# Reordering pair products and operand sums in blocks 1 to 3 and 6 of an attention and GeGLU kernel

## The chip, the core and the metric

The kernel runs on one core of one Trainium2 chip. The metric is the device time of one execution in microseconds; lower is better. Before the change it is 294.11 us, the median of three runs (294.11 to 294.32). The profile of one such run spans 292.1 us from its first to its last instruction.

## What is computed

Linear attention over 8 batches, 8 heads, 576 positions and a head width of 64, followed by a gated feed-forward layer on 4608 rows:

```python
q_s = softmax(q, over the head width)
k_s = softmax(k, over the positions)
kv  = einsum('bhsd,bhse->bhde', k_s, v)
x   = einsum('bhsd,bhde->bhse', q_s, kv)      # reshaped to 4608 x 512
g   = x @ w_gate                              # 512 x 1536
val = x @ w_val                               # 512 x 1536
out = (gelu(g) * val) @ w_out                 # 1536 x 512
```

## The kernel before

A batch is a **block** of 512 rows; the remaining 64 rows of all eight batches are gathered into block 8 (`B`). The blocks run in the order 0 to 6, 8, 7. While the feed-forward of block b runs on TensorE (PE), the attention of block b + 1 is prepared on the other engines: DVE (VectorE), ACT (ScalarE) and POOL (GpSimd).

From block 2 on, most of `x @ w_gate` and `x @ w_val` is done as a Strassen-Winograd scheme: the rows of x are cut into two halves of 256, and two columns of 128 hidden units, k and k + 3, form a **pair**. Seven products of four 128x256 matmuls take the place of eight. A column that is not in a pair is done plainly, as two **halves** (`g` and `v`) of four 128x512 matmuls. The scheme needs four sums of x (`xs`), four of the weights, and, for the output product, sums of the hidden values (`sh`, `s4` and in place in `ht`).

The order of one block is a string. `k.i` is step i of pair k, `8g` and `8v` are the two halves of column 8, letters are places where other work rides along:

```python
FOUR = ("a 7g l 7v n 0.1 6.1 0.2 6.2 0.3 6.3 m p 10g 0.4 6.4 1.1 t 10v 1.2 s0 8g u0 1.3 8v 1.4 2.1"
        " 11g 2.2 11v 2.3 s1")                                 # blocks 2, 3: four pairs
FIVE = ("a 8g l 8v n m 0.1 6.1 0.2 6.2 0.3 6.3 0.4 1.1 p 6.4 7.1 t 1.2 7.2 1.3 s0 7.3 2.1 1.4 u0 11g 2.2"
        " y 7.4 11v 2.3 s1")                                   # blocks 4 to 6: five pairs
SIX = ("0.1 6.1 0.2 6.2 0.3 6.3 0.4 1.1 6.4 7.1 s0 1.2 7.2 1.3 u0 7.3 1.4 2.1 7.4 8.1 2.2"
       " 8.2 2.3 s1 8.3 2.4")                                  # blocks 8, 7: six pairs
```

The four steps of a pair use three PSUM tiles, `pga`, `pgb` and `pgc`. What reads a tile has to be done before the next product is added to it:

```python
if i == 1:
    product_gv(1, pa, ...)          # PE
    nc.scalar.copy(out=pb, in_=pa)  # ACT: seed of pb
    product_gv(5, pc, ...)
    s5 = snap(pc, b >= B - 1 or b > 3 and k % NO == 1)   # on DVE if true, else ACT
elif i == 2:
    product_gv(6, pa, ...)          # adds to pa: waits for the seed copy
    s2 = snap(pa)                   # ACT
    product_gv(3, pc, ...)          # adds to pc: waits for s5
    add(cc[:, 0], pc, s2)           # DVE
elif i == 3:
    product_gv(7, pa, ...)          # waits for s2
    add(cc[:, 1], pa, s5)           # DVE
    product_gv(2, pb, ...)
    final(pb, k)                    # ACT gelu, then DVE product into ht
    ... upper(cc)                   # ACT gelu, then POOL (for pair 8 DVE) product into ht
else:
    product_gv(4, pa, ...)          # waits for add(cc[:, 1], pa, s5)
    final(pa, k + 3)
```

The sums of x are four chained subtractions on POOL: `t0 = b12 - b11`, `t1 = b22 - t0`, `t2 = b22 - b12`, `t3 = b21 - t1`. Product 5 reads `t0`, product 6 `t1`, product 7 `t2` and product 4 `t3`; products 1, 2 and 3 read x itself.

The places `a` and `n` each bring `norm_pair`, a DVE reduction and a reciprocal for the next block's softmax; `a`, `m` and `p` bring its multiplications on POOL.

The output product of a block (`out_strassen`) is seven products of twelve 128x256 matmuls on the tiles `psa`, `psb` and `psc`:

```python
product(1, ps["a"]); s1 = snap("a")         # ACT or DVE
product(2, ps["b"]); add("b", s1, 0, 0)     # DVE
product(5, ps["c"]); s5 = snap("c")
product(6, ps["a"]); s2 = snap("a")         # waits for s1
product(3, ps["c"]); add("c", s2, 0, 1)     # waits for s5
product(7, ps["a"]); add("a", s5, 1, 1)     # waits for s2
... attention product of the next block, its casts to xt, sum_x
product(4, ps["a"]); yo = copy of psa       # waits for the add; ACT
```

Of the kernel before, what the change touches and what calls it, by code (L numbers as in the profile page):

```python
# [18 lines left out]
def kernel(  # L19
# [60 lines left out]
    def big(shape, dt, name, hold=False, seed=False):  # L80
        tag = ring.pop(next(i for i, x in enumerate(ring) if x in full) if seed else 0)
        t = ps_big.tile(shape, dt, name=name, tag=tag)
        words = 1
        for n in shape[1:]:
            words *= n
        (full.add if words == 512 and shape[0] == 128 and dt == f32 else full.discard)(tag)
        if hold:
            held[id(t)] = (t, tag)
        else:
            ring.append(tag)  # L90
        return t
# [484 lines left out]
    def sum_h(j0, j1, which, eng="dve"):  # L576
        step = 1 if j0 in (0, 4) and j1 < NO + (j0 > 0) else NO // 2
        js, ks = slice(j0, j1, step), slice(NO + j0, NO + j1, step)
        a11, a21 = ht[:, js, 0:256], ht[:, js, 256:512]
        a12, a22 = ht[:, ks, 0:256], ht[:, ks, 256:512]  # L580
        s1, s2 = sh[1][:, js], sh[2][:, js]
        for i in which:
            o, a, b, op = {1: (s1, a21, a22, ALU.add), 2: (s2, s1, a11, ALU.subtract),
                           3: (a21, a11, a21, ALU.subtract),
                           4: (s4[:, js], a12, s2, ALU.subtract)}[i]
            (nc.gpsimd if eng == "pool" else nc.vector).tensor_tensor(out=o, in0=a, in1=b, op=op)  # L586
# [17 lines left out]
    def sum_w1(i, k, eng):  # L604
# [5 lines left out]
                       3: (a21, a11, a21, ALU.subtract), 4: (t[2], a12, t[1], ALU.subtract)}[i]  # L610
        (nc.gpsimd if eng == "pool" else nc.vector).tensor_tensor(out=o, in0=a, in1=b, op=op)

    def sum_x(xt, xs=xs):
        b11, b12, b21, b22 = (xt[:, c:c + 2, r:r + 256] for c in (0, 2) for r in (0, 256))
        t = [xs[:, i] for i in range(4)]
        for o, a, b in ((t[0], b12, b11), (t[1], b22, t[0]), (t[2], b22, b12), (t[3], b21, t[1])):
            nc.gpsimd.tensor_tensor(out=o, in0=a, in1=b, op=ALU.subtract)

    def product_gv(i, ps, xt, k, first):
        lo, hi = slice(k * P, (k + 1) * P), slice((k + NO // 2) * P, (k + NO // 2 + 1) * P)  # L620
        xs = xs_b[xt is st.get((B - 1, "xt"))]
        for t, w, nm in ((0, wv_sb, "v"), (1, wg_sb, "g")):
# [8 lines left out]

    FOUR = ("a 7g l 7v n 0.1 6.1 0.2 6.2 0.3 6.3 m p 10g 0.4 6.4 1.1 t 10v 1.2 s0 8g u0 1.3 8v 1.4 2.1"
            " 11g 2.2 11v 2.3 s1")
    FIVE = ("a 8g l 8v n m 0.1 6.1 0.2 6.2 0.3 6.3 0.4 1.1 p 6.4 7.1 t 1.2 7.2 1.3 s0 7.3 2.1 1.4 u0 11g 2.2"
            " y 7.4 11v 2.3 s1")
    SIX = ("0.1 6.1 0.2 6.2 0.3 6.3 0.4 1.1 6.4 7.1 s0 1.2 7.2 1.3 u0 7.3 1.4 2.1 7.4 8.1 2.2"
           " 8.2 2.3 s1 8.3 2.4")
    steps = {b: (SIX if b >= B - 1 else FIVE if b > 3 else FOUR).split() for b in range(2, B + 1)}  # L640
    live = {}

    def half(b, xt, c, nm):
        t = big([P, 512], f32, "ps" + nm)
# [8 lines left out]
    def pair_step(b, xt, k, i):  # L653
        def final(ps, fi):
            gl = ffn.tile([P, 256], f32, name="glq", tag="gl")
            nc.scalar.activation(out=gl, in_=ps[:, 1], func=ACTF.Gelu)  # L656
            nc.vector.scalar_tensor_tensor(out=ht[:, fi, 0:256], in0=ps[:, 0], scalar=_H_SCALE,  # L657
                                           in1=gl, op0=ALU.mult, op1=ALU.mult)
            let_go(ps)

        def snap(ps, dve=False):
            sn = ffn.tile([P, 2, 256], f32, name="snq", tag="snq")
            if dve:
                nc.vector.tensor_scalar(out=sn, in0=ps, scalar1=_H_SCALE, scalar2=None, op0=ALU.mult)
            else:
                nc.scalar.activation(out=sn, in_=ps, func=ACTF.Copy, scale=_H_SCALE)  # L666
            return sn

        def add(o, ps, sn):
            nc.vector.scalar_tensor_tensor(out=o, in0=ps, scalar=_H_SCALE, in1=sn,  # L670
                                           op0=ALU.mult, op1=ALU.add)

        def upper(cc):
            nc.scalar.activation(out=cc[:, :, 1], in_=cc[:, :, 1], func=ACTF.Gelu,  # L674
                                 scale=1.0 / _H_SCALE)
            (nc.vector if k == NFI - NO // 2 - 1 else nc.gpsimd).tensor_tensor(  # L676
                out=ht[:, k:k + NO // 2 + 1:NO // 2, 256:512], in0=cc[:, :, 0], in1=cc[:, :, 1],
                op=ALU.mult)

        if i == 1:  # L680
            live["odd"] = odd = not live.get("odd", True)
            cc = cc_b[b > 2] if odd else ffn.tile([P, 2, 2, 256], f32, name="cc", tag="cc", bufs=1)
            pa = big([P, 2, 256], f32, "pga", True)
            product_gv(1, pa, xt, k, True)
            pb = big([P, 2, 256], f32, "pgb", True, True)
            nc.scalar.copy(out=pb, in_=pa)  # L686
            pc = big([P, 2, 256], f32, "pgc", True)
            product_gv(5, pc, xt, k, True)
            live[k] = [cc, pa, pb, pc, snap(pc, b >= B - 1 or b > 3 and k % NO == 1)]
            return  # L690
        cc, pa, pb, pc, s5 = live[k]
        if i == 2:
            product_gv(6, pa, xt, k, False)
            s2 = snap(pa)
            product_gv(3, pc, xt, k, False)
            add(cc[:, 0], pc, s2)
            let_go(pc)
        elif i == 3:
            product_gv(7, pa, xt, k, False)
            add(cc[:, 1], pa, s5)  # L700
            product_gv(2, pb, xt, k, False)
            final(pb, k)
            if k == NFI - NO // 2 - 1 or 3 < b < B - 1 and k < 2 or 3 < b < B - 1 and k == NO:
                live["late"] = lambda: upper(cc)
            elif 3 < b < B - 1 and k == NO + 1:
                live["y"] = lambda: upper(cc)
            else:
                upper(cc)
        else:
            product_gv(4, pa, xt, k, False)  # L710
            if steps[b] and steps[b][0].endswith(".1"):
                live["late"] = lambda: final(pa, k + NO // 2)
            else:
                final(pa, k + NO // 2)
# [15 lines left out]
            if late:  # L730
                late()

    SUMS = {9: (0, 4, (1, 2)), 10: (0, 4, (3, 4))}

    def product(i, ps, first, ts=(0, 1), js=range(NO)):
        for j in js:
# [15 lines left out]
    def last_js(b):  # L752
        return (NO - 2 if b < 2 else NO // 2 - 1, NO)

    def out_strassen(b, last):
# [30 lines left out]

        js = (0, 1, 2, 3, 4, 5) if b < 2 else (0, 3, 1, 4, 2, 5)
        get("a")
        four = 1 < b < B - 1
        cut = 3 if four else 4  # L790
        product(1, ps["a"], True, js=js[:cut])
        if four:
# [2 lines left out]
        ride(b, NS, 0)  # L795
        if b < 4:
            ride(b, PR, "u1")
        if b >= B - 1:
            pair_step(b, get_x(b), NFI - NO // 2 - 1, 4)
        get("b")  # L800
        product(1, ps["a"], False, js=js[4:])
# [11 lines left out]
        for x in tiles_["b"]:  # L813
            let_go(x)
        sum_h(*last_js(b), (4,), "pool" if b > 1 else "dve")
        get("c")
        product(5, ps["c"], True, js=js)
        sum_h(*last_js(b), (3,), "pool" if b > 1 else "dve")
# [22 lines left out]
        if b == B:  # L841
            go_on(B - 1, get_x(B - 1), 1)
        product(4, ps["a"], False, js=js)
        nc.scalar.activation(out=yo[1][:, :, c[0]], in_=tiles_["a"][0], func=ACTF.Copy,
                             scale=1.0 / _H_SCALE)
        let_go(tiles_["a"][0])
# [101 lines left out]
    def at(b, kind, i, *fns):  # L948
        plan.setdefault((b, kind, i), []).extend(fns)
# [37 lines left out]
    for i, x in enumerate(("g1", "v1", "g2", "v2", "g4", "v4")):  # L987
        at(0, FI, 5 + i, L(sum_wgv, x[0], int(x[1])))
    at(0, FI, NFI - 2, L(sum_w, 1))
    at(1, NS, 1, L(sum_wgv, "g", 3))  # L990
    at(1, NS, 2, L(sum_wgv, "v", 3))
    for b in range(2, B):
        n = b + 1
        if n < B:
# [8 lines left out]
            at(b, PR, "e", L(exp, "q", n + 1), L(exp, "k", n + 1))  # L1003
    at(4, PR, "l", load_rem0)
    at(4, PR, "e", exp_rem0)
    at(5, NS, 1, norm_rem0)
    at(6, PR, "t", L(unit_trem, 0))
    for b in range(2, B - 1):
        n = b + 1
        at(b, NS, 4, L(unit_x4, n, ("act", "dve"), 0 if n == B - 1 else None))  # L1010
        at(b, NS, 0, L(unit_kv4, n, True))
        if b < 6:
            at(b, NS, 4, L(preload, ACTF.Gelu))
        at(b, NS, 4, L(lambda n: sum_x(get_x(n)), n if n < B - 1 else B))
    at(B, NS, 2, L(lambda: sum_x(get_x(B - 1), xs_b[1])))
    for b in range(2, B + 1):
        for j in range(NO // 2 - 1):
            at(b, PR, f"s{j}", L(sum_h, j, NO, (1,)))
            if j and b > 3:
                at(b, PR, f"u{j}", L(sum_h, j, NO, (2, 3, 4)))  # L1020
            else:
                at(b, PR, f"s{j}", L(sum_h, j, NO, (3,), "pool"))
                at(b, PR, f"u{j}", L(sum_h, j, NO, (2,)), L(sum_h, j, NO, (4,), "pool"))
    for b, kind, i, dk, x in ((1, FI, 6, 0, 1), (1, FI, 6, 0, 2), (1, FI, 6, 0, 4), (1, FI, 9, 0, 3),
                              (2, NS, 1, 1, 1), (2, NS, 1, 1, 2), (3, NS, 2, 1, 4), (3, NS, 2, 1, 3),
                              (4, NS, 2, 2, 1), (4, NS, 2, 2, 2), (6, NS, 1, 2, 4), (6, NS, 2, 2, 3)):
        at(b, kind, i, L(sum_w1, x, NO + dk, "pool" if b < 3 else "dve"))


    def ride(b, kind, i):  # L1030
# [65 lines left out]
```

The softmax here doesn't subtract the row's maximum and nothing guards it: scores larger than these inputs give would overflow.

## Time and profile before

| | busy us | share of the span |
|---|---|---|
| PE (matmuls) | 281.8 | 96% |
| DVE | 229.2 | 78% |
| POOL | 200.2 | 69% |
| ACT | 198.1 | 68% |

The page divides the span into 40 slices and gives each engine's busy share in tenths. TensorE's granted clock is full in all of them. A group of the page is a source line, an engine and an operation with the tiles it writes and reads, the shape, the count, and the busy time; L471 is the plain half, L629 a pair's product, L745 the output product, L586 a sum of hidden values, L670 a pair's add, L238 the reduction of the softmax, L617 a sum of x, L466 the dummy gelu that makes ACT load its table. Matmuls are pipelined, so that one starts before the last one's shown end; the distance from start to start is the pace. In the timeline a line has the start, the duration, engine, source line and operation, the tiles, and in brackets the idle time before it with what ended it.

By stretches, TensorE is busy for 29.10 of the 29.30 us from 53.0 to 82.3 (most of block 1), 30.14 of 30.40 in block 2 (82.3 to 112.7), 30.43 of 31.20 in block 3 (112.7 to 143.9), and all of the 29.60 us of blocks 4 and 5 each. Block 6 runs from 203.1 to about 233.

### The profile page before, as it was taken

What the parts mean: (1) busy time and instruction counts of PE and PEld (TensorE: products, weight loads), DVE (VectorE), ACT (ScalarE), POOL (GpSimd) and SP (SyncE); (2) the same over time, 40 slices, a digit from 0 to 9 for tenths busy, and PEclk for the clock granted to TensorE, in tenths of its full rate; (3) what the DMA queues carried; (4) which work ended last, traced back from release to release, by engine and by line L of the source; (5) the groups of instructions that cost most, each with busy time, mean ns of one, the idle gap of its engine ahead of it and who ended that gap; (6) DMA issues with size and microseconds to landing.
All of it is one profiled execution on the core that took longest, in us unless ns stands there. A gap on an engine that the chain in (4) does not pass through costs nothing.

```text
span 292.1 us, 6496 instructions
## 1 busy us (share of the span) xinstructions
PE 281.8 (96%) x2497; PEld 207.5 (71%) x2497; DVE 229.2 (78%) x426; ACT 198.1 (68%) x332; POOL 200.2 (69%) x184
## 2 busy tenths in 40 slices
PE   3999999999999999999999999999999999999994
PEld 1444445445777786768688878887888888888883
DVE  2954888868997678669988889887889779938992
ACT  3763367785697688766887698769774477537650
POOL 1567746986478589976996689759975476283640
PEclk9999999999999999999999999999999999999999
DMA  6999999998059903990189318921240110033003
GB/s 217 374 381 388 400 392 390 354 342 236 3 165 375 183 2 137 345 239 2 72 271 323 74 74 274 312 67 53 93 83 19 72 75 0 3 73 73 2 0 144
DMA packets 54622, 51.72 MB, mean 177 GB/s; under 512 B 18496, under 2 KB 50496, under 8 KB 54592
## 3 DMA queue, kind: packets, MB, share of 16 engines
q1 hardware_dynamic: 52864, 49.49, 54.1%
q10 hardware_dynamic: 1728, 1.84, 1.9%
q8 instruction: 19, 0.31, 0.4%
q14 instruction: 11, 0.09, 0.1%
HBM read 37.75 MB, written 9.44 MB: 162 GB/s over the span
## 4 chain that ended last, share of the span: by engine, by line
PE 87%; DVE 4%; POOL 4%; DMA 2%; ACT 1%; issue 1%; POOLq 0%; ACTq 0%
PE pga L629 21%; PE psa L745 12%; PE psg L471 11%; PE psv L471 10%; PE pgc L629 10%; PE psc L745 6%; PE pgb L629 5%; PE psy L539 4%; PE psb L745 2%; DMA qt<-in_q_dram 2%; DVE sh L586 2%; PE pskv L347 2%; POOL s L586 1%; POOL v L186 1%; PE psx L434 1%
## 5 line engine op out<-in xcount | busy, mean ns | idle before, releaser
L629 PEld LDWEIGHTS <-wgv_sb 128*128 128x128 f16 x560 | 54.3, 98 | 11.2 <-issue 0.8
L471 PEld LDWEIGHTS <-wgv_sb 128*128 128x128 f16 x304 | 29.5, 98 | 30.3 <-issue 0.7
L248 POOL TENSOR_TENSOR eq<-eq,rrq 128x640 f16<-128x640 f16 (+1 forms) x27 | 34.8, 1306 | 11.3 <-DVE rrq L240 7.3
L745 PEld LDWEIGHTS <-ht 128*128 128x128 f16 x384 | 36.6, 98 | 7.8 <-issue 2.5
L471 PE MATMUL psg<-xt,wgv_sb 128*128 128x512 f16 x152 | 41.1, 379 | 0.0
L471 PE MATMUL psv<-xt,wgv_sb 128*128 128x512 f16 x152 | 41.0, 379 | 0.0
L676 POOL TENSOR_TENSOR ht<-eq 128x512 f16<-128x512 f32 x17 | 21.7, 1274 | 22.4 <-ACT eq L674 22.4
L629 PE MATMUL pga<-xs,wgv_sb 128*128 128x256 f16 x232 | 34.5, 272 | 0.2 <-DVE cc L670 0.2
L586 POOL TENSOR_TENSOR s<-ht,sh 128x512 f16<-128x512 f16 x16 | 18.7, 1172 | 13.9 <-DVE sh L586 13.9
L656 ACT ACTIVATE glq<-pgb 128x256 f32<-128x256 f32 x35 | 13.3, 381 | 21.1 <-PE pgb L629 14.4
L657 DVE SCALAR_TENSOR_TENSOR ht<-pga,glq 128x256 f16<-128x256 f32 x35 | 14.8, 422 | 14.2 <-ACT glq L656 14.0
L586 POOL TENSOR_TENSOR ht<-ht 128x512 f16<-128x512 f16 x16 | 19.2, 1197 | 8.7 <-DVE sh L586 8.7
L476 ACT ACTIVATE gl<-psg 128x512 f32<-128x512 f32 x24 | 13.8, 598 | 16.6 <-PE psg L471 16.5
L186 POOL CAST v<-vt 128x640 f16<-128x640 f32 x26 | 19.1, 777 | 8.1 <-PE pskv L347 6.4
L477 DVE SCALAR_TENSOR_TENSOR ht<-psv,gl 128x512 f16<-128x512 f32 x24 | 16.0, 686 | 10.0 <-PE psv L471 8.2
L686 ACT COPY pgb<-pga 128x512 f32<-128x512 f32 x35 | 20.4, 582 | 5.1 <-PE pga L629 4.8
L745 PE MATMUL psa<-tw,ht 128*128 128x256 f16 x192 | 23.4, 272 | 0.1
L666 ACT ACTIVATE snq<-pga 128x512 f32<-128x512 f32 x35 | 20.9, 600 | 3.5 <-PE pga L629 3.2
L210 ACT ACTIVATE ek<-kt 128x1280 f16<-128x1280 f32 (+1 forms) x11 | 19.1, 1748 | 6.1 <-DMA kt<-in_k_dram 4.2
L676 POOL TENSOR_TENSOR ht<-cc 128x512 f16<-128x512 f32 x16 | 20.4, 1272 | 2.8 <-ACT cc L674 2.8
L238 DVE TENSOR_REDUCE rq<-eq 128x20 f32<-128x1280 f16 (+1 forms) x12 | 17.2, 1432 | 4.4 <-ACT eq L210 4.4
L745 PEld LDWEIGHTS <-sh 128*128 128x128 f16 x192 | 18.7, 98 | 2.3
(173 smaller groups left out, 685.2 us busy)
## 6 DMA issues: line engine op xcount, KB each, us to landing
out_dram<-yo SPq DMA_DIRECT2D x15, 512.0 KB, 3.4
kt<-in_k_dram SPq DMA_DIRECT2D x7, 640.0 KB, 9.0
vt<-in_v_dram SPq DMA_DIRECT2D x7, 640.0 KB, 5.9
qt<-in_q_dram SPq DMA_DIRECT2D x7, 640.0 KB, 7.7
qt<-in_q_dram SPq DMA_DIRECT2D x8, 512.0 KB, 8.4
wost<-in_moe_w_out_dram SPq DMA_DIRECT2D x6, 512.0 KB, 7.9
kt<-in_k_dram SPq DMA_DIRECT2D x6, 512.0 KB, 9.6
vt<-in_v_dram SPq DMA_DIRECT2D x6, 512.0 KB, 6.5
```

The source lines that it names most:

```text
L186: nc.gpsimd.tensor_copy(out=dst, in_=src)
L210: nc.scalar.activation(out=dst[:, n0:NC, h0 * D:h1 * D].rearrange(o, d=D, **({"t": 2} if b >= QUAD else {})), in_=heads(tiles[(nm, b)], b, ...
L238: nc.vector.reduce_sum(rq, e, axis=mybir.AxisListType.X)
L248: (nc.gpsimd if eng == "pool" else nc.vector).tensor_tensor(out=e, in0=e, in1=rrq.unsqueeze(-1).to_broadcast((P, n, 2, D)), op=ALU.mult)
L471: nc.tensor.matmul(ps, w[:, ci, fi * P:(fi + 1) * P], xt[:, ci, :], start=(ci == 0), stop=(ci == HP - 1))
L477: nc.vector.scalar_tensor_tensor(out=ht[:, fi, :], in0=psv, scalar=_H_SCALE, in1=gl, op0=ALU.mult, op1=ALU.mult)
L586: (nc.gpsimd if eng == "pool" else nc.vector).tensor_tensor(out=o, in0=a, in1=b, op=op)
L629: nc.tensor.matmul(ps[:, t], a, x, start=(first and t == 0 and c == 0), stop=(c == 1), skip_group_check=True)
L666: nc.scalar.activation(out=sn, in_=ps, func=ACTF.Copy, scale=_H_SCALE)
L676: (nc.vector if k == NFI - NO // 2 - 1 else nc.gpsimd).tensor_tensor(out=ht[:, k:k + NO // 2 + 1:NO // 2, 256:512], in0=cc[:, :, 0], in1=c ...
L686: nc.scalar.copy(out=pb, in_=pa)
L745: nc.tensor.matmul(ps[t], a, w, start=(first and j == js[0] and (t == ts[0] or ps[t].tensor is not ps[ts[0]].tensor)), stop=(j == js[-1]), ...
```

## The change

It has four parts. In blocks 1 to 3 some operand sums move behind work that TensorE waits for sooner, and some go from POOL to DVE. In block 6 the two plain columns 8 and 11 become a sixth pair. So that TensorE has work before the sums of x are ready, the first two products of that block need x alone (step `k.0` is the first half of step `k.1`), and six steps of block 6 are issued ahead of the copy that evacuates block 5's last accumulator. The sums of x of block 6 are divided between POOL and DVE. The weight sums that the sixth pair needs are made in block 5, and what stood in their place there, the reduction of the leftover rows (`norm_rem0`), moves into the pairs of block 5.

```diff
+    def sum_x6():
+        xt = get_x(6)
+        b11, b12, b21, b22 = (...)
+        for eng, o, a, b in ((nc.gpsimd, 0, b12, b11), (nc.vector, 1, b22, xs[:, 0]), (nc.vector, 2, b22, b12),
+                             (nc.gpsimd, 3, b21, xs[:, 1])):
+            eng.tensor_tensor(out=xs[:, o], in0=a, in1=b, op=ALU.subtract)
...
-    FOUR = ("a 7g ... 1.1 t 10v 1.2 s0 8g u0 1.3 8v 1.4 2.1"
+    FOUR = ("a 7g ... 1.1 t 10v 1.2 8g 1.3 s0 8v u0 1.4 2.1"
...
+    SIX6 = ("0.0 6.0 0.1 6.1 a 0.2 6.2 n 0.3 6.3 m 0.4 1.1 6.4 p 7.1 t 1.2 7.2 1.3 s0 7.3 u0 1.4 2.1 7.4 8.1 2.2"
+            " 8.2 2.3 8.3 s1 2.4")
...
-        if i == 1:
+        if i == 1 and k in begun:
+            cc, pa, pb = begun.pop(k)
+        elif i < 2:
             ... product 1 and the seed copy
+            if i == 0:
+                begun[k] = (cc, pa, pb)
+                return
+        if i == 1:
             ... product 5 and its snapshot
...
-            if k == NFI - NO // 2 - 1 or 3 < b < B - 1 and k < 2 or 3 < b < B - 1 and k == NO:
+            if k == NFI - NO // 2 - 1 or 3 < b < B - 1 and (k < 2 or k == NO or b == 6):
                 live["late"] = lambda: upper(cc)
...
-    SUMS = {9: (0, 4, (1, 2)), 10: (0, 4, (3, 4))}
+    SUMS = {9: (0, 4, (1, 2)), 10: (0, 4, (3,)), 11: (0, 4, (4,))}
...
-        four = 1 < b < B - 1
+        four = 1 < b < B - 2
...
-        if b >= B - 1:
+        if b >= B - 2:
             pair_step(b, get_x(b), NFI - NO // 2 - 1, 4)
...
         sum_h(*last_js(b), (4,), "pool" if b > 1 else "dve")
+        ride(b, PR, "r1")
         get("c")
...
         product(4, ps["a"], False, js=js)
+        if b == 5:
+            go_on(6, get_x(6), 6)
         nc.scalar.activation(out=yo[1][:, :, c[0]], in_=tiles_["a"][0], func=ACTF.Copy, ...)
...
-    at(1, NS, 1, L(sum_wgv, "g", 3))
-    at(1, NS, 2, L(sum_wgv, "v", 3))
+    at(1, NS, 2, L(sum_wgv, "g", 3), L(sum_wgv, "v", 3))
...
-    at(5, NS, 1, norm_rem0)
+    at(5, PR, "u0", norm_rem0)
...
-        at(b, NS, 4, L(lambda n: sum_x(get_x(n)), n if n < B - 1 else B))
+        at(b, NS, 4, sum_x6 if n == 6 else L(lambda n: sum_x(get_x(n)), n if n < B - 1 else B))
...
-                at(b, PR, f"s{j}", L(sum_h, j, NO, (3,), "pool"))
-                at(b, PR, f"u{j}", L(sum_h, j, NO, (2,)), L(sum_h, j, NO, (4,), "pool"))
+                if j:
+                    at(b, PR, "r1", L(sum_h, j, NO, (3,), "pool"))
+                    at(b, PR, "u1", L(sum_h, j, NO, (2, 4)))
+                else:
+                    ... as before
...
-                              (2, NS, 1, 1, 1), (2, NS, 1, 1, 2), (3, NS, 2, 1, 4), (3, NS, 2, 1, 3),
-                              (4, NS, 2, 2, 1), (4, NS, 2, 2, 2), (6, NS, 1, 2, 4), (6, NS, 2, 2, 3)):
-        at(b, kind, i, L(sum_w1, x, NO + dk, "pool" if b < 3 else "dve"))
+                              (2, NS, 2, 1, 1), (2, NS, 2, 1, 2), (3, NS, 2, 1, 4), (3, NS, 2, 1, 3),
+                              (4, NS, 2, 2, 1), (4, NS, 2, 2, 2), (5, NS, 2, 2, 4), (5, NS, 2, 2, 3)):
+        at(b, kind, i, L(sum_w1, x, NO + dk, "pool" if b < 2 else "dve"))
```

More of the change, by code (lines that the diff above doesn't have):

```diff
@@ L611, in sum_w1 @@
         (nc.gpsimd if eng == "pool" else nc.vector).tensor_tensor(out=o, in0=a, in1=b, op=op)
+    def sum_x6():
+        xt = get_x(6)
+        b11, b12, b21, b22 = (xt[:, c:c + 2, r:r + 256] for c in (0, 2) for r in (0, 256))
+        for eng, o, a, b in ((nc.gpsimd, 0, b12, b11), (nc.vector, 1, b22, xs[:, 0]), (nc.vector, 2, b22, b12),
+                             (nc.gpsimd, 3, b21, xs[:, 1])):
+            eng.tensor_tensor(out=xs[:, o], in0=a, in1=b, op=ALU.subtract)
     def sum_x(xt, xs=xs):
@@ L630, in product_gv @@
                                  skip_group_check=True)
-    FOUR = ("a 7g l 7v n 0.1 6.1 0.2 6.2 0.3 6.3 m p 10g 0.4 6.4 1.1 t 10v 1.2 s0 8g u0 1.3 8v 1.4 2.1"
+    FOUR = ("a 7g l 7v n 0.1 6.1 0.2 6.2 0.3 6.3 m p 10g 0.4 6.4 1.1 t 10v 1.2 8g 1.3 s0 8v u0 1.4 2.1"
             " 11g 2.2 11v 2.3 s1")
@@ L637 @@
             " y 7.4 11v 2.3 s1")
+    SIX6 = ("0.0 6.0 0.1 6.1 a 0.2 6.2 n 0.3 6.3 m 0.4 1.1 6.4 p 7.1 t 1.2 7.2 1.3 s0 7.3 u0 1.4 2.1 7.4 8.1 2.2"
+            " 8.2 2.3 8.3 s1 2.4")
     SIX = ("0.1 6.1 0.2 6.2 0.3 6.3 0.4 1.1 6.4 7.1 s0 1.2 7.2 1.3 u0 7.3 1.4 2.1 7.4 8.1 2.2"
            " 8.2 2.3 s1 8.3 2.4")
-    steps = {b: (SIX if b >= B - 1 else FIVE if b > 3 else FOUR).split() for b in range(2, B + 1)}
-    live = {}
+    steps = {b: (SIX if b >= B - 1 else SIX6 if b == 6 else FIVE if b > 3 else FOUR).split() for b in range(2, B + 1)}
+    live, begun = {}, {}
     def half(b, xt, c, nm):
@@ L1021 @@
             else:
-                at(b, PR, f"s{j}", L(sum_h, j, NO, (3,), "pool"))
-                at(b, PR, f"u{j}", L(sum_h, j, NO, (2,)), L(sum_h, j, NO, (4,), "pool"))
+                if j:
+                    at(b, PR, "r1", L(sum_h, j, NO, (3,), "pool"))
+                    at(b, PR, "u1", L(sum_h, j, NO, (2, 4)))
+                else:
+                    at(b, PR, "s0", L(sum_h, j, NO, (3,), "pool"))
+                    at(b, PR, "u0", L(sum_h, j, NO, (2,)), L(sum_h, j, NO, (4,), "pool"))
     for b, kind, i, dk, x in ((1, FI, 6, 0, 1), (1, FI, 6, 0, 2), (1, FI, 6, 0, 4), (1, FI, 9, 0, 3),
-                              (2, NS, 1, 1, 1), (2, NS, 1, 1, 2), (3, NS, 2, 1, 4), (3, NS, 2, 1, 3),
-                              (4, NS, 2, 2, 1), (4, NS, 2, 2, 2), (6, NS, 1, 2, 4), (6, NS, 2, 2, 3)):
-        at(b, kind, i, L(sum_w1, x, NO + dk, "pool" if b < 3 else "dve"))
+                              (2, NS, 2, 1, 1), (2, NS, 2, 1, 2), (3, NS, 2, 1, 4), (3, NS, 2, 1, 3),
+                              (4, NS, 2, 2, 1), (4, NS, 2, 2, 2), (5, NS, 2, 2, 4), (5, NS, 2, 2, 3)):
+        at(b, kind, i, L(sum_w1, x, NO + dk, "pool" if b < 2 else "dve"))
     def ride(b, kind, i):
```

## The prediction, made before the result was known

> **What bounds the kernel now.** I read the page's busy shares and slices first. "PE" is the matmul engine, TensorE.
>
> ```profile
> PE 281.8 (96%) x2497; PEld 207.5 (71%) x2497; DVE 229.2 (78%) x426; ACT 198.1 (68%) x332; POOL 200.2 (69%) x184
> ...
> PE   3999999999999999999999999999999999999994
> ```
>
> TensorE is busy in every slice but the ends, and no other engine is near it. So time can only leave by fewer matmul columns or by shorter TensorE stalls. The second view is TensorE's own waits.
>
> ```profile
> PE psc L745 <- POOL s L586: 0.5, 2, 0.3
> PE pgc L629 <- POOL xs L617: 0.3, 1, 0.3
> PE pga L629 <- DVE cc L670: 0.2, 1, 0.2
> ...
> PE psb L745 <- DVE ht L477: 0.2, 1, 0.2
> ```
>
> These understate what is lost, since a matmul's shown end trails its successor's start. The third view, the timeline, lets me count start to start: four 128x512 matmuls take 0.864 us, four 128x256 (one product) 0.437 us, and whatever lies beyond that between two starts is lost.
>
> ```profile
> 106.22 1.47 PE L745 MATMUL psa<-tw,sh 128*128 128x256 f16 x12
> 107.95 1.25 PE L745 MATMUL psc<-wo_sb,s 128*128 128x256 f16 x10 [0.26 <-POOL s L586]
> ...
> 114.36 0.60 PE L629 MATMUL pga<-xt,wgv_sb 128*128 128x256 f16 x4
> 115.24 0.38 PE L629 MATMUL pgc<-xs,wsv 128*128 128x256 f16 x2 [0.28 <-POOL xs L617]
> ...
> 126.12 1.03 PE L471 MATMUL psv<-xt,wgv_sb 128*128 128x512 f16 x4
> 127.39 0.38 PE L629 MATMUL pga<-xs,wgv_sb 128*128 128x256 f16 x2 [0.24 <-DVE cc L670]
> ```
>
> 106.22 + 12 x 0.109 = 107.53, the next start is 107.95: 0.42 lost. 114.36 + 0.437 against 115.24: 0.44 lost. 126.12 + 0.864 against 127.39: 0.41 lost. In the same way the timeline gives 0.33 at 73.0 (block 1), 0.12 at 96.1 (block 2) and 0.42 at 138.7 (block 3). From block 4 to the end nothing but switches of about 0.1 us is lost. All that the reordering of blocks 1 to 3 can give is these **2.1 us**.
>
> **What the Trainium skill says.** "TensorE: Matmul & The Clock Gate", section "Back-to-back issue gap", gives 518 cycles for 512 columns and 262 for 256; at its 2.4 GHz 216 and 109 ns. The trace agrees: 0.864/4 and 0.437/4. "Perfetto Trace Analysis", section "Tensor Engine Instruction (MATMUL, LD_WEIGHTS)", says that ACT, DVE and GpSimd are strict FIFO: an instruction that is ready stands behind one that isn't. My main step rests on this; no engine's timeline here shows an overtaking. "VectorE: DVE Perf Modes", section "The perf-mode tier table (the rule you actually need)", has tensor_reduce at 1x only; the 128x1280 reductions take 1.47 us here. "GPSIMD Engine Reference", section "Specifications", says that GpSimd shares its SBUF interfaces with DVE and contends with DVE instructions that have two SBUF inputs. The trace shows it: the sum that takes 0.42 us alone takes 1.24 beside GpSimd work (DVE `sh`, 103.83 and 105.44).
>
> **Part 1, blocks 1 to 3.** I went through each wait with the order in which the changed program puts instructions on each engine.
>
> Block 1, 73.0: the last gate (`ht` L477, 0.68) now goes ahead of the sum `s` (0.68), so the second operand of product 2 is there in time: 0.33 gone. But DVE works without a pause from here to 80.81, and product 6 waits for its snapshot (`sn`, 74.92 before, 74.80 now), and product 4 of the block for `yo<-psa` at DVE's end. The two weight sums moved behind the snapshot free one wait of 0.12 and return at that end. I count **0.15**.
>
> Blocks 2 and 3, the fourth product of pair 1 (96.1 and 127.3): the add that releases its PSUM tile stood behind two sums. In block 3 the add can now start at 125.89 instead of 126.66 and ends 126.57, before TensorE asks at 126.98. **0.12 + 0.41** gone.
>
> Blocks 2 and 3, third output product (107.5 and 138.7): the trace names `s` on POOL, but the first matmul also needs the snapshot `sn<-psc`, which ended at 107.90.
>
> ```profile
> 103.83 1.24 DVE L586 TENSOR_TENSOR sh<-sh,ht 128x512 f16<-128x512 f16 x1
> 104.99 0.41 DVE L586 TENSOR_TENSOR sh<-ht 128x512 f16<-128x512 f16 x1
> 105.44 1.26 DVE L586 TENSOR_TENSOR sh<-sh,ht 128x512 f16<-128x512 f16 x1
> 106.62 0.68 DVE L783 SCALAR_TENSOR_TENSOR yo<-psb,sn 128x512 f32<-128x512 f32 x1
> 107.23 0.67 DVE L777 TENSOR_SCALAR sn<-psc 128x512 f32<-128x512 f32 x1
> ```
>
> Two sums are stretched by 0.8 us each by POOL's sums beside them. Those POOL sums leave: one `s` goes to DVE (0.42), one `ht` goes behind. Then 103.83 + four sums of 0.42 = 105.51, the add to 106.11, and the snapshot starts when product 5 is done (106.43) and ends at 107.11. POOL's last `s` ends at 106.71. **0.42 + 0.42** gone.
>
> Block 3's first product 5 (115.24): POOL's queue ahead of `xs` loses one `s` and two weight sums (3 x 1.16), so `xs` is bound by its input (ACT, 111.83 on the shifted clock) and four casts, and ends near 113.4; TensorE asks at 114.4. **0.44** gone. DVE gets the two weight sums, about 0.4 to 0.9 each beside the casts; they end just before the add on `psa` may start.
>
> Sum: 0.15 + 0.12 + 0.42 + 0.44 + 0.41 + 0.42 = **1.96 us gained**.
>
> **Part 2, block 5.** The reduction of the leftover rows (0.67) and its reciprocal (0.19) go ahead of a sum and the add that the fourth product of pair 2 waits for. In block 4's and 5's order that add already sets the start (ends 192.46, product at 192.51). Laid out with the traced durations it ends at 192.75: **0.29 lost**.
>
> **Part 3, block 6.** Two plain columns are 16 matmuls of 512: 4 x 0.864 = 3.46 us. A pair is 7 products: 3.06. **0.40 gained.** The price is the order on ACT and DVE. The opening of block 6 before:
>
> ```profile
> 202.71 1.28 ACT L466 ACT_TABLE_LOAD   x1
> 204.01 0.20 ACT L466 ACTIVATE tiny<-tiny 128x1 f32<-128x1 f32 x1
> ...
> 203.59 1.47 DVE L238 TENSOR_REDUCE rq<-eq 128x20 f32<-128x1280 f16 x1
> 205.10 0.28 DVE L240 RECIPROCAL rrq<-rq 128x20 f32<-128x20 f32 x1
> ...
> 205.88 1.48 DVE L238 TENSOR_REDUCE rq<-eq 128x20 f32<-128x1280 f16 x1
> ```
>
> Before, two plain columns (203.05 to 204.81) covered this load and both reductions were over before the first add at 208.11. Now the pairs start at 203.05. First products of pairs 0 and 6 run to 203.92; `xs` 0 ends at 203.93 on POOL, so product 5 starts at 203.98: 0.06 lost. ACT is free at 204.12 and does two seed copies and two snapshots with 0.5 us from start to start, so the snapshot of pair 0's `pgc` ends at 205.70, but product 3 asks at 205.30: **0.45 lost**.
>
> Then the second reduction. It now stands in DVE's queue between the adds of pair 0/6's product 3 and those of their product 7. Let X be the moment pair 6's product 6 has been issued. ACT's snapshot of it starts at X + 0.25 and ends at X + 0.85; the DVE add (0.69) ends at X + 1.57; the reduction (1.47) at X + 2.96; its reciprocal (0.28) at X + 3.28; only then the add on pair 0's `pga` (0.68), done at X + 3.87. TensorE has five products until it wants to add product 4 to that tile: X + 5 x 0.437 = X + 2.19. It gets it at X + 3.92. **1.73 lost.** This is the largest single term.
>
> Further on, block 6 now gives ACT six pairs, four of them with the snapshot on ACT, and the gelu of pair 7 stands ahead of pair 2's copies. Continuing with the same durations I get pair 8's seed copy 0.18 late, its snapshots 0.05 and 0.34, and the last add 0.17: **0.6 to 0.8 lost**, less the 0.1 that this place lost before. This tail I trust least.
>
> Sum of block 6: 0.06 + 0.45 + 1.73 + 0.75 - 0.10 - 0.40 = **2.5 us lost**.
>
> Total: 294.11 - 1.96 + 0.29 + 2.5 = **294.9 us**.
>
> **The rivals.** A: the waits in block 6 stay hidden, because something gives that I took as fixed. Then the gains stand alone: 294.11 - 1.96 - 0.40 = 291.8. For it speaks that blocks 7 and 8 run six pairs without a stall in this trace; against it, that they have no reductions and all `pgc` snapshots on DVE. B: the waits of blocks 1 to 3 move on instead of going, since DVE is at 78% and receives work from POOL; with half the gain back and block 6 as above, 295.9. For it speaks block 1's unbroken DVE queue. C: PSUM space. Six tiles of pairs 0 and 6 are open while the fifth block's last accumulator still waits for its copy, seven of eight banks; that copy goes behind six ACT instructions, but the next tile of pair 7 needs it only some 4 us later, so I give it nothing.
>
> **Range and chances.** The gain of part 1 is sound to some 0.5 us and the loss in block 6 to about 1. I take 293.2 to 295.9. A's full gain is 0.8% and B's loss 0.6%, so beyond 2% either way there is next to nothing.
>
> **What would show it.** Right: TensorE's waits no longer list `s`, `xs` or `ht` L477; a wait of `pga` (fourth product) for a DVE add of 1 us or more early in block 6, with a TENSOR_REDUCE directly ahead of that add; a wait of `pgc` for ACT's snapshot just before; a larger wait in block 5 near 192. Wrong: block 6 without such a wait (rival A), or new waits on DVE in blocks 2 and 3 (rival B).

## The result, and the profile after

The changed kernel takes **296.39 us** (median of four runs, 296.33 to 296.54). The kernel before took 294.22 us beside it, and the ratio is 1.0074, with a 95% interval of 1.0057 to 1.0092. It is slower by 2.2 us, where 0.8 was predicted (294.9 against 294.11), and lies above the stated range of 293.2 to 295.9. The profiled run spans 294.6 us at full clock.

The busy shares and slices of the profile after:

```profile
PE 282.2 (96%) x2509; PEld 208.4 (71%) x2509; DVE 231.7 (79%) x435; ACT 199.4 (68%) x336; POOL 193.6 (66%) x178
...
PE   3999999999999999999999999989799999999994
```

The shares hardly move. The row of slices does: two slices, 191.5 to 198.9 and 206.2 to 213.6 us, are no longer full. TensorE's waits after, without those of the warm-up (what waits, for what; total us, times, longest):

```profile
PE pga L636 <- DVE cc L679: 1.5, 1, 1.5
PE psa L760 <- DVE ht L666: 1.1, 1, 1.1
PE pgc L636 <- ACT snq L675: 0.3, 1, 0.3
PE pga L636 <- ACT snq L675: 0.2, 1, 0.2
PE psa L760 <- DVE yo L798: 0.2, 1, 0.2
```

The waits for `s`, for `xs` and for `ht` L477 are gone. Two large ones have come: a pair's fourth product for DVE's add, and the output product for a gate. The last line is the end of block 1.

**Blocks 1 to 3** as the timeline of TensorE after shows them, in the order of the lines shown of before:

```profile
106.01 1.47 PE L760 MATMUL psa<-tw,sh 128*128 128x256 f16 x12
107.32 1.25 PE L760 MATMUL psc<-wo_sb,s 128*128 128x256 f16 x10
...
113.73 0.60 PE L636 MATMUL pga<-xt,wgv_sb 128*128 128x256 f16 x4
114.17 0.38 PE L636 MATMUL pgc<-xs,wsv 128*128 128x256 f16 x2
...
125.06 1.03 PE L471 MATMUL psv<-xt,wgv_sb 128*128 128x512 f16 x4
125.92 0.60 PE L636 MATMUL pga<-xs,wgv_sb 128*128 128x256 f16 x4
```

The distances from start to start are 1.31, 0.44 and 0.86: twelve or four matmuls at full pace, nothing lost. DVE in block 2 shows why:

```profile
103.61 0.41 DVE L586 TENSOR_TENSOR sh<-sh,ht 128x512 f16<-128x512 f16 x1
104.06 0.42 DVE L586 TENSOR_TENSOR s<-ht,sh 128x512 f16<-128x512 f16 x1
104.40 0.42 DVE L586 TENSOR_TENSOR sh<-ht 128x512 f16<-128x512 f16 x1
104.85 0.42 DVE L586 TENSOR_TENSOR sh<-sh,ht 128x512 f16<-128x512 f16 x1
105.19 0.69 DVE L798 SCALAR_TENSOR_TENSOR yo<-psb,sn 128x512 f32<-128x512 f32 x1
106.21 0.69 DVE L792 TENSOR_SCALAR sn<-psc 128x512 f32<-128x512 f32 x1 [0.33 <-PE psc L760]
```

No sum is stretched, and the snapshot starts as soon as product 5 is done. The first matmul of block 4's output product starts at 162.14 before and at 160.25 after: 1.89 us are gained by there.

**Block 5** is where the prediction failed. TensorE before, and the sum `sh` on DVE that matters below:

```profile
191.77 0.82 PE L745 MATMUL psa<-wo_sb,ht 128*128 128x256 f16 x6
192.51 0.60 PE L629 MATMUL pga<-xs,wgv_sb 128*128 128x256 f16 x4
...
194.01 0.61 PE L745 MATMUL psa<-wo_sb,ht 128*128 128x256 f16 x4
...
192.78 0.41 DVE L586 TENSOR_TENSOR sh<-ht 128x512 f16<-128x512 f16 x1
```

and TensorE after:

```profile
189.88 0.82 PE L760 MATMUL psa<-wo_sb,ht 128*128 128x256 f16 x6
190.83 0.60 PE L636 MATMUL pga<-xs,wgv_sb 128*128 128x256 f16 x4
...
192.33 0.39 PE L760 MATMUL psa<-wo_sb,ht 128*128 128x256 f16 x2
193.79 0.39 PE L760 MATMUL psa<-wo_sb,ht 128*128 128x256 f16 x2 [1.08 <-DVE ht L666]
```

At the fourth product of pair 2 (`pga`) 0.09 us were lost before; after, 0.30 are lost there (TensorE asks near 190.5). At the last two matmuls of output product 1, where nothing was lost before, **1.24 us are lost at 192.5**. The chain of work that ended last, in that stretch (start, us, what):

```profile
187.54 0.59 DVE rq L275
...
188.16 0.21 DVE rrq L277
...
188.44 0.27 POOL eq0r L278
188.71 0.81 issue
189.51 1.15 POOL s L586
190.66 1.24 POOL ht L685
...
191.93 1.48 DVE sh L586
193.40 0.34 DVE ht L666
193.75 0.05 issue
193.79 0.39 PE psa L760 x2
```

Read from below: TensorE waits for the gate `ht`, which stands in DVE's queue behind the sum `sh`. That sum waits for POOL's product into `ht`, which stands in POOL's queue behind `s` and behind the multiplication `eq0r`, the third part of `norm_rem0`. (The chain gives `eq0r` 0.27 us and calls the rest "issue"; POOL's timeline has 1.11 us for it, from 188.44 on, up to the start of `s`.) And the sum takes 1.48 us in place of 0.41: POOL's next product into `ht` began at 191.86, 0.07 us before it.

**Block 6**, DVE's timeline and then TensorE's product that waits for it:

```profile
207.01 0.69 DVE L679 SCALAR_TENSOR_TENSOR eq<-pgc,snq 128x512 f32<-128x512 f32 x1
207.62 1.48 DVE L238 TENSOR_REDUCE rq<-eq 128x20 f32<-128x1280 f16 x1
209.13 0.28 DVE L240 RECIPROCAL rrq<-rq 128x20 f32<-128x20 f32 x1
209.33 0.63 DVE L679 SCALAR_TENSOR_TENSOR cc<-pga,snq 128x512 f32<-128x512 f32 x1
...
210.01 0.61 PE L636 MATMUL pga<-xs,wgv_sb 128*128 128x256 f16 x4 [1.48 <-DVE cc L679]
```

The second reduction stands ahead of the add, as predicted. TensorE's pace from 207.93 would have put this product at 208.37, so 1.65 us are lost (from unrounded starts).

### The profile page after: what moved, and what is told of

Same layout as the page of the kernel before. It is cut to its first block, busy times and chain, and to the rows that moved or that the text cites. A ratio compares the mean times of both kernels' runs of the same rounds, so it can differ in the third digit from the quotient of the medians.

```text
span 294.6 us, 6525 instructions
## 1 busy us (share of the span) xinstructions
PE 282.2 (96%) x2509; PEld 208.4 (71%) x2509; DVE 231.7 (79%) x435; ACT 199.4 (68%) x336; POOL 193.6 (66%) x178
## 4 chain that ended last, share of the span: by engine, by line
PE 87%; DVE 5%; POOL 2%; ACT 2%; issue 2%; ACTq 1%; POOLq 0%
PE pga L636 19%; PE psa L760 13%; PE psg L471 10%; PE psv L471 10%; PE pgc L636 10%; PE psc L760 7%; PE pgb L636 4%; PE psb L760 4%; PE psy L539 4%; PE pswarm L463 2%; PE pskv L347 1%; POOL ht L685 1%; DVE yo L798 1%; ACT L466 1%; POOL s L586 1%
## 5 line engine op out<-in xcount | busy, mean ns | idle before, releaser
L685 POOL TENSOR_TENSOR ht<-cc 128x512 f16<-128x512 f32 x18 | 23.2, 1288 | 25.3 <-ACT cc L683 25.3
L471 PE MATMUL psg<-xt,wgv_sb 128*128 128x512 f16 x144 | 39.0, 379 | 0.0
L471 PE MATMUL psv<-xt,wgv_sb 128*128 128x512 f16 x144 | 38.9, 379 | 0.0
L636 PE MATMUL pga<-xs,wgv_sb 128*128 128x256 f16 x240 | 35.7, 273 | 1.9 <-DVE cc L679 1.5
L586 POOL TENSOR_TENSOR s<-ht,sh 128x512 f16<-128x512 f16 x14 | 16.2, 1155 | 18.3 <-DVE sh L586 18.3
L186 POOL CAST v<-vt 128x640 f16<-128x640 f32 x26 | 19.8, 803 | 7.7 <-PE pskv L347 6.2
L477 DVE SCALAR_TENSOR_TENSOR ht<-psv,gl 128x512 f16<-128x512 f32 x24 | 16.0, 686 | 10.1 <-PE psv L471 8.4
L685 POOL TENSOR_TENSOR ht<-eq 128x512 f16<-128x512 f32 x15 | 19.1, 1274 | 4.2 <-ACT eq L683 4.2
```

What stands on the lines that cost most here:

```text
L186: nc.gpsimd.tensor_copy(out=dst, in_=src)
L471: nc.tensor.matmul(ps, w[:, ci, fi * P:(fi + 1) * P], xt[:, ci, :], start=(ci == 0), stop=(ci == HP - 1))
L477: nc.vector.scalar_tensor_tensor(out=ht[:, fi, :], in0=psv, scalar=_H_SCALE, in1=gl, op0=ALU.mult, op1=ALU.mult)
L636: nc.tensor.matmul(ps[:, t], a, x, start=(first and t == 0 and c == 0), stop=(c == 1), skip_group_check=True)
```

## The experiments

In each run the kernel before ran beside the others on the same chip (medians 294.16 to 294.28 on the three chips used). "Lost" means start to start beyond TensorE's pace.

**1. Blocks 1 to 3 alone.** Everything of blocks 5 and 6 is taken back.

```diff
-SIX6 if b == 6 else FIVE
+FIVE
...
-    at(5, PR, "u0", norm_rem0)
+    at(5, NS, 1, norm_rem0)
...
-... (5, NS, 2, 2, 4), (5, NS, 2, 2, 3)
+... (6, NS, 1, 2, 4), (6, NS, 2, 2, 3)
```

> Only the part in blocks 1 to 3 of the change is kept; blocks 5 and 6 stand as before the change. Theory: all that was lost lies in blocks 5 and 6, and the reordering gained about 1.9 us at TensorE, as the two traces show from block 1 to block 4 (block 4's fourth product of pair 2 starts 1.9 us earlier). So 294.2 - 1.9 = 292.3 us, and TensorE waits for nothing of 0.3 us or more after the start, but the one at the end of block 1. Rival: the gain of blocks 1 to 3 is partly given back by DVE further on, and block 5's new wait is a late effect of it: then 293 us or more.

Measured: **292.11 us**, ratio 0.993 (0.9913 to 0.9946), 2.10 us less than the 294.21 of the kernel before. This version beats both kernels. All that the change loses lies in blocks 5 and 6: 296.39 - 292.11 = 4.28 us.

**2. The leftover rows' sum back in its place**, the rest as after:

```diff
-    at(5, PR, "u0", norm_rem0)
+    at(5, NS, 1, norm_rem0)
```

> The changed kernel with one thing undone: the reduction of the leftover rows, its reciprocal and its POOL multiplication go back to where they were, behind block 5's sixth output product. Theory: that move alone makes the two waits near 190.4 and 192.5 us (0.2 and 1.24 us more than before), so 296.4 - 1.45 = 294.95 us. Rival: the wait at 192.5 comes from the weight sums that came into block 5 or from the steps of block 6 that are issued ahead; then it stays, and less than 0.3 us is gained.

Measured: 296.46 us. Nothing was gained, against the expectation. Yet the trace has no loss left at 190 and 192; it has a new one of 2.04 us at the end of block 5. (The traced execution is the slowest of four, 297.87 us against 296.37 to 296.55, and in it TensorE's granted clock was 0.50 from 202.31 to 205.72; the loss of 2.04 lies ahead of that.)

**3. Only its multiplication back.** The reduction stays among the pairs; POOL multiplies later.

```diff
     # norm_rem0, at (5, PR, "u0"): reduction and reciprocal only
-    nc.gpsimd.tensor_tensor(out=e, in0=e, in1=rrq..., op=ALU.mult)
+at(5, NS, 1, mul_rem0)          # the same instruction, later
```

> The changed kernel, in which the leftover rows' reduction and reciprocal stay on DVE ahead of block 5's sum, and only their multiplication on POOL (1.1 us) goes back behind the sixth output product. Theory: the 1.24 us wait at 192.5 is POOL's: the multiplication makes the product into ht that the sum sh of pairs 1 and 4 waits for 1.1 us late, and the sum then starts beside POOL's next instruction and takes 1.48 in place of 0.42 us. So 1.24 goes and the 0.2 us at 190.4 stays: 296.4 - 1.24 = 295.15 us. Rival: DVE's own queue, longer by 0.86 us, is the cause: then less than 0.4 us is gained.

Measured: 296.45 us, again no gain. But this trace divides the loss in block 5. The one at 192.5 is gone, and the 0.30 at 190.4 is still there. DVE's timeline where the long sum was:

```profile
191.11 0.42 DVE L590 TENSOR_TENSOR sh<-ht 128x512 f16<-128x512 f16 x1
...
191.91 0.42 DVE L670 SCALAR_TENSOR_TENSOR ht<-pga,glq 128x256 f16<-128x256 f32 x1 [0.37 <-ACT glq L669]
```

So the reduction on DVE costs 0.30 - 0.09 = 0.21 us (I had 0.29 for it), and the multiplication on POOL, with the reduction where it is, the 1.24 that I had not counted. Without it `s` starts at 188.70 instead of 189.51 and `sh` at 191.11 instead of 191.93, and `sh` takes 0.42 instead of 1.48: 0.8 us are the delay itself and 1.06 the stretch, of which some was slack. The gain went into a new wait, seen in the timelines of DVE, POOL and TensorE of this run:

```profile
197.48 2.85 DVE L615 TENSOR_TENSOR kt<-wgv_sb,kt 128x512 f16<-128x512 f16 x1
200.25 0.93 DVE L615 TENSOR_TENSOR wgv_sb<-wgv_sb 128x512 f16<-128x512 f16 x1
201.11 0.68 DVE L802 SCALAR_TENSOR_TENSOR yo<-psa,sn 128x512 f32<-128x512 f32 x1
...
198.01 2.89 POOL L186 CAST v<-vt 128x640 f16<-128x640 f32 x4
...
201.84 0.92 PE L764 MATMUL psa<-tw,ht 128*128 128x256 f16 x7 [1.76 <-DVE yo L802]
```

The first weight sum takes 2.85 us beside POOL's multiplication and casts; in the kernel after it began in the first cast and took 0.49. Behind it stands the add `yo` that frees the output accumulator, and product 4 comes 1.92 us late. A part of this is no further loss: the wait behind the table load shrinks from 0.46 to 0.12 us, since the load is now over before TensorE comes to block 6. The next two runs test whether the casts did it.

**4. Weight sums to POOL in block 6**, together with edit 2:

```diff
-... (5, NS, 2, 2, 4), (5, NS, 2, 2, 3)):
+... (6, PR, "a", 2, 4), (6, PR, "a", 2, 3)):     # on POOL, not DVE
```

> The kernel after, with the sum of the leftover rows back behind the snapshot of output product 5 (as in the run leftover_sum_back) and with the two weight sums of block 5 moved as well: from DVE at the end of block 5 to GpSimd in block 6, where it stands idle from 208.56 to 210.75. My theory: in leftover_sum_back the 1.45 us of block 5 were gained, and a DVE weight sum beside GpSimd's casts (2.90 us instead of 0.49) made a new wait of 2.04 of them. Without that sum the gain stays: 296.39 - 1.45 = 294.95 (294.6 to 295.3). Rival: the reduction of the leftover rows itself (0.67 and 0.19), standing ahead of a snapshot, makes the wait at the end of block 5; then it stays and the time is 296.4.

Measured: **294.94 us** (ratio to before 1.0025, 1.0014 to 1.0035). The rival falls: the reduction of the leftover rows is in the same place as in run 2, and TensorE loses nothing from 190 to 202 but the switches of 0.1 us that the kernel before has too. With this, block 5 is priced: 296.39 - 294.94 = **1.45 us**. What is left over run 1, 294.94 - 292.11 = 2.83, is block 6.

**5. The casts moved instead.** Edit 2, weight sums left on DVE, POOL's four casts moved to block 6:

```diff
-at(5, NS, 2, L(cast_v, 7, 0, H))
+at(6, PR, "a", L(cast_v, 7, 0, H))
```

> The kernel after with the sum of the leftover rows back behind the snapshot of output product 5, as in leftover_sum_back (296.46), and the weight sums left on DVE at the end of block 5; only GpSimd's four casts of v beside them are moved to block 6, behind its two multiplications. If the casts stretched the weight sum (2.90 us instead of 0.49), it now takes 0.4 to 1.0 us, the wait of 2.04 at the end of block 5 goes, and the time is that of weight_sums_pool: 294.9 (294.6 to 295.4, with up to 0.5 for GpSimd's later work in block 6). Rival: the DVE work itself (reduction 0.67, reciprocal 0.19, two weight sums) is too much ahead of the add that frees the accumulator; then a wait of 1 us or more stays there and the time is 296 or more.

Measured: 295.11 us (294.87 to 295.34), within 0.2 of run 4, which lacks a loss of 0.14 that this run has at 214.8. DVE's timeline, at the same two sums:

```profile
197.51 0.92 DVE L611 TENSOR_TENSOR kt<-wgv_sb,kt 128x512 f16<-128x512 f16 x1
198.35 0.41 DVE L611 TENSOR_TENSOR wgv_sb<-wgv_sb 128x512 f16<-128x512 f16 x1
```

From the start of the first to the end of the second are now 1.25 us, where run 3 had 3.70; what is left of the first one's stretch falls beside the multiplication `eq0r`, which ends at 198.15. The casts were the cause of the wait in runs 2 and 3.

**6. Block 6 without the second reduction.** Heads 4 to 7 of block 7 take the reciprocals of heads 0 to 3; the reduction and its reciprocal are left out, so this is no version to use.

```diff
+        if b == 7 and g == 1:
+            for j in range(2): st[(b, "norm", 2 + j)] = (..., st[(b, "norm", j)][1], n)
+            return
```

> The changed kernel without the second softmax reduction and its reciprocal in block 6 (1.47 + 0.28 us on DVE; head pairs 2 and 3 of block 7 are scaled with the reciprocals of pairs 0 and 1, so part of the output is not the reference's). Theory: this reduction, ahead of the add on pair 0's pga in DVE's queue, is the 1.65 us stall of block 6; without it the add ends some 0.03 us after TensorE asks, so 296.4 - 1.6 = 294.8 us. Rival: the reduction only fills a wait that something else sets (ACT's snapshots, the adds themselves), and half or more of the stall stays: 295.6 us or more.

Measured: 294.87 us, 1.52 less than after. The 1.65 at the fourth product is gone, and 0.23 comes up at a later add. My largest term is confirmed.

**7. The second reduction one step later**, otherwise as after:

```diff
-... a 0.2 6.2 n 0.3 6.3 m 0.4 ...
+... a 0.2 6.2 0.3 6.3 n m 0.4 ...
```

> The kernel after, with block 6's second reduction one step later, behind the two adds on pga and their gates. My theory: the wait of 1.65 us is that of the fourth product for an add that stands behind the reduction, so it goes, and little comes back (the next snapshot on DVE is asked for some 2.4 us after its product): 296.39 - 1.65 + 0.2 = 294.9 (294.6 to 295.3), as when the reduction is left out (294.87). Rival: DVE has no room in block 6 (busy 3.64 of the 4 us from 208 to 212), so the 1.76 us only move on to the snapshot of pair 1: 296 or more.

Measured: 295.46 us (295.3 to 295.59): 0.93 less than after, between the two theories. The 1.65 is gone, and 0.44 and 0.38 come back. DVE and then TensorE in this run:

```profile
209.65 1.47 DVE L238 TENSOR_REDUCE rq<-eq 128x20 f32<-128x1280 f16 x1
211.16 0.28 DVE L240 RECIPROCAL rrq<-rq 128x20 f32<-128x20 f32 x1
211.35 0.63 DVE L673 TENSOR_SCALAR snq<-pgc 128x512 f32<-128x512 f32 x1
...
212.03 0.38 PE L636 MATMUL pgc<-xt,wsv 128*128 128x256 f16 x2 [0.28 <-DVE snq L673]
...
213.28 0.60 PE L636 MATMUL pgc<-xt,sh 128*128 128x256 f16 x4 [0.22 <-DVE snq L673]
```

Now pair 1's and pair 7's snapshots stand behind the reduction.

**8. Edits 4 and 7 together.**

> Both of the changes just named. If the two costs are separate waits they add: 296.39 - 1.45 - 1.65 + 0.2 = 293.5 (293.0 to 293.9). If a later wait takes one back: 294.9.

Measured: 294.66 us (294.46 to 294.94, 20 executions), only 0.28 below run 4. Beside the 0.44 and 0.38, a third loss of 0.55 appears: DVE's add into the buffer `eq` waits until POOL has read that buffer, and POOL is late by the two weight sums (run 7, which leaves them on DVE, has no loss there). DVE's line, and POOL's that it waits for:

```profile
213.21 0.69 DVE L679 SCALAR_TENSOR_TENSOR eq<-pgc,snq 128x512 f32<-128x512 f32 x1 [0.84 <-POOL ht L685]
...
211.90 1.28 POOL L685 TENSOR_TENSOR ht<-eq 128x512 f16<-128x512 f32 x1
```

**9. And two snapshots from ACT to DVE**, those of pairs 0 and 8:

```diff
-snap(pc, b >= B - 1 or b > 3 and k % NO == 1)
+snap(pc, b >= B - 1 or b > 3 and k % NO == 1 or b == 6 and k in (0, 8))
```

> As before, and the snapshots of pairs 0 and 8 in block 6 on DVE instead of ACT. The wait of 0.46 behind the table load goes (the DVE snapshot can start at 204.3 and end at 205.0, product 3 asks at 205.30), and of the 0.9 at 219.6 to 222.9, which are ACT's queue, some 0.5: 293.5 - 0.46 - 0.5 = 292.5 (292.0 to 293.0). Rival: the DVE snapshot puts the first reduction and the adds behind it 0.7 us later, and the gain at 204.7 returns as a wait there: 293.2.

Measured: 294.99 us, no better than run 8. The 0.46 behind the table load is gone, as expected, but 0.39 returns at an add 2.5 us later, as the rival had it, and the loss at the buffer `eq` grows from 0.55 to 1.12. Of the 0.9 near 219 to 222, of which I expected some 0.5 to go, a loss of 0.33 goes, but the last one, at an add, grows from 0.26 to 0.54.

**10. The second reduction far later**, with edit 4 and without edit 9:

```diff
-... 0.2 6.2 n 0.3 6.3 m 0.4 1.1 6.4 p 7.1 t ... s0 7.3 u0 1.4 2.1 7.4 8.1 2.2
+... 0.2 6.2 0.3 6.3 0.4 1.1 6.4 7.1 ... s0 7.3 u0 n 1.4 2.1 7.4 8.1 m p t 2.2
```

> Both changes (leftover sum back, weight sums on GpSimd in block 6), and block 6's second reduction far later: behind the sums of u0, where DVE stood idle for 1.06 and 0.86 us (216.74 to 217.80 and 218.22 to 219.08 in the run both), its two multiplications on GpSimd behind the fifth product of pair 8. In the run both, the reduction behind the gates of pair 0 and 6 cost 0.44 and 0.38 us at the snapshots of pairs 1 and 7, and 0.55 at an add that waited for GpSimd. If DVE is simply full in the opening of block 6 and free later, these three go and at most 0.5 comes back: 294.66 - 1.37 + 0.4 = 293.7 (293.2 to 294.1). Rival: DVE's later work is as tight, a wait of the same size comes up near 219 to 224, and the time is 294.6 or more.

Measured: **293.54 us**, ratio to before 0.9975 (0.9965 to 0.9984). DVE's timeline at the reduction's new place:

```profile
215.53 1.47 DVE L238 TENSOR_REDUCE rq<-eq 128x20 f32<-128x1280 f16 x1
```

The three losses of run 8 shrink to one of 0.15 us. The whole is faster than the kernel before only because of what blocks 1 to 3 gain; against run 1, with five pairs, the sixth pair still costs 293.54 - 292.11 = 1.43 us. What is still lost (0.46 at the table load, about 1.2 in ACT's later queue and at its end) is more than the 0.40 that the sixth pair saves in matmul columns. An arrangement in which the sixth pair pays was not found.

## Why the prediction was wrong, point by point

- **Part 1 was right**: 1.96 us predicted, 1.89 by block 4 in the trace, 2.10 as a version of its own. Blocks 2 and 3 went as laid out. Block 1 gave little, as said (from 67.7 us on it is 0.17 shorter, where I had 0.15): 0.33 was gained at the output product's second operand, and part came back behind it (0.17 is lost at 74.6, and 0.31 instead of 0.20 at 80.2).
- **Part 2 is the step that failed**: "Laid out with the traced durations it ends at 192.75: 0.29 lost". Measured, 1.45. I followed DVE's queue and counted only `norm_rem0`'s reduction and reciprocal there; these did cost 0.21. Its third instruction, the multiplication on POOL, I left out, as if nothing stood behind it in POOL's queue. It holds back `s` and the product into `ht`, and through them a sum on DVE that stands ahead of a gate (run 3). This term alone takes the total to 296.1, above the range; the tail of part 3 alone would have left it inside, at 295.3. My sign "a larger wait in block 5 near 192" came true for the large wait by luck: I meant the fourth product of pair 2, where 0.30 is lost.
- **The sum's own duration was mis-sized with it.** I took 0.42 us for `sh`, as traced before, when POOL was idle beside it. The delay brought it next to a POOL instruction, and it took 1.48. I had used this very effect for part 1 and not asked where the change would create it.
- **Part 3 was right in kind and nearly in size**: 2.5 predicted, 2.83 between runs 4 and 1. The opening 0.06 and 0.45 came as 0.06 and 0.46, the second reduction's 1.73 as 1.65. The tail, for which I had 0.75, is the term that was too small: 0.26, 0.09, 0.33, 0.27 and 0.16 make 1.11. What sets each of these I read from the trace; no run tests them one by one.
- **The rivals**: A (the waits stay hidden) and B (part 1 given back) did not happen. B's figure of 295.9 is near the result for another reason than its own. I had no rival for part 2 at all, which is why the range was too narrow.

The sum, with what was measured in the place of the two wrong terms: 294.9 + (1.45 - 0.29) + (1.11 - 0.75) = 296.4. That it closes to 0.1 us is in part luck: the gain of blocks 1 to 3 (2.10 for 1.96) and the time of the kernel before (294.22 for 294.11) were off too, and cancel.

## What to carry to other kernels

When work is moved, follow every one of its instructions into its own engine's queue, and in each ask who stands behind it and who waits for that; here a small operation on an engine that is a third idle cost six times as much as the reduction it belonged to (1.24 against 0.21 us). A duration taken from the trace holds only beside the neighbours it had there, so ask what the move puts side by side, above all a two-input sum on DVE and POOL's sums, products and casts. And an edit that removes a wait and gains nothing has not refuted the cause: look in its trace for the next wait before giving up the theory (runs 2 and 4).

## What the runs showed of the hardware

A two-input DVE sum of 128x512 took 0.42 us alone, 1.48 when it began just behind the start of one POOL instruction, and 2.85 in run 3. There it began at 197.48, inside POOL's multiplication, and ended at 200.33, after three of the casts that follow the multiplication. The Trainium skill, "SBUF — State Buffer", section "SBUF: two separate sides", says that the one of the two engines that starts first holds the ports they share as an exclusive lock for a whole instruction, and that the other one blocks. The 1.48 agrees: POOL's instruction ends at 193.12, the sum at 193.40, 0.28 later; in run 5 the weight sum ends 0.28 after the multiplication beside it (198.43 and 198.15), and in run 3 0.28 after the third cast (200.33 and 200.05). From block 2 on, every DVE sum of this size that took 0.7 us or more in the traces of before, after and runs 3 and 5 ends 0.27 to 0.28 us after the end of a POOL instruction.

The 2.85 goes further than the skill's sentence: the sum had begun before these casts (198.01, 198.67 and 199.34), and they still went first. It is not so behind every POOL instruction that another follows at once: in the kernel after, a sum begun at 138.06 came through behind one, ahead of the cast after it, and took 0.90; and the weight sum of 0.49 began inside the first cast and came through behind it. Why it did not in run 3 is not shown.
